# Two more pairs of a two-layer fp32 chain in seven products: first layer's pairs 3 and 4 in two phases, products summed in PSUM

## The chip, the cores and the metric

One core of one Trainium2 chip. The time is that of one execution on the device, in microseconds, median over several. TensorE (PE) multiplies; ScalarE (ACT) and VectorE (DVE) read and write what PE leaves in PSUM; GpSimd (POOL) only fills small tiles; SyncE (SP) issues every DMA from one queue, in order. Each engine works through its own list in the order in which it was built.

## The reference

```
q_s = exp(q - max(q, -1)) / (sum + 1e-9)          # over the head's 64 columns
k_s = exp(k - max(k, axis=2)) / (sum + 1e-9)      # over the 576 positions
x   = q_s @ (k_s^T @ v)                           # 8 batches, 8 heads, 576 x 64
x   = [4608, 512]                                 # heads side by side
h   = x @ w_in1 ; g = h * sigmoid(1.702 h) ; x = g @ w_out1     # 512 -> 2048 -> 512
h   = x @ w_in2 ; g = max(0.01 h, h)       ; x = g @ w_out2
```

q, k and v are float32; the four weight matrices come as float64 and are turned into float32 on the chip. All of it is kept at float32 accuracy.

## The kernel before

The 4608 rows are nine chunks of 512 (0 to 8). Float32 factors are cut into a high and a low half (`split_hi` on ACT, `split_lo` on DVE) and each 128x128x512 product is made of three matmuls: high-high, low-high, high-low. A hidden stripe of 128 columns is an f (0 to 15), two of them a quad (n = 0 to 7).

Layer 1 (index 0 in the code) begins with chunks 0 and 1, one after the other, while attention and weight conversion run beside them. Then come pairs of chunks: pair 2 (chunks 2 and 3), pair 3 (4, 5), pair 4 (6, 7), and chunk 8 alone (`single`). Layer 2 has four pairs and chunk 8 alone. For a pair, the first product takes seven products of blocks for eight (Winograd's form of Strassen): the pair is cut into a11, a12, a21, a22, s1 to s4 are sums of these, and the weights' sums t1 to t4 are built once and stored (`wq`).

There are two ways to run a pair. In layer 1, `pair_first` makes the quads (`quad_step`, line 896) and, beside each, the second product of the first chunk (`g2`, line 789, eight of eight blocks); `pair_second` then makes the second chunk's second product. A quad step is 42 matmuls of L732 and 24 of L789. In layer 2, `quad_apart` (line 947) makes all quads alone, keeping g of both chunks in SBUF, and `pair_apart` then makes the second product in seven rounds (`ROUNDS`) of four pages, each page 12 matmuls (L1056): 336 for a pair instead of 384. For each page `prepare` casts a high half (ACT `sh`), subtracts for the low half (DVE `sl`), and in the first three rounds makes one more DVE subtraction for a later round.

Attention goes by units (chunk c, pair of heads j), pipelined over three ticks by class `Units`, one tick beside each quad: `kma` and `kmb` (transposes for the column maximum), `qtp` (transposes of q), `kvp` (k^T v), `pxt` (the product with q), with q's exponentials on ACT (`q1b`) and k's maximum and subtraction on DVE. Weights of layer 2 are converted by `conv_step`, 33 steps of two ACT and four DVE instructions (L109, L112; L116, L117, L126, L130), spread over layer 1's pairs 3 and 4.

PSUM has eight banks: three named h, acc0 to acc3, and one named att. In `quad_step` the first block a goes to SBUF (`p`, L905) and DVE adds it to b and c (L900). A gap list (`gaps[0..9]`) says beside which block each extra piece is issued, and a scheduler then orders each engine's list.

## Time and profile before

| | us |
|---|---|
| median of three runs | 1624.9 (1624.11 to 1628.83) |
| the profiled execution | 1628.65 |
| its span | 1626.9 |
| PE busy in the span | 1587.7 |
| first quad of pair 3 begins | 440.79 |
| first quad of pair 4 begins | 634.19 |
| first matmuls of chunk 8's first product (`h`) | 807.50 |

PE is busy in almost all of the span after the first 200 us. A busy PE says only that matmuls are in flight; whether it is at its pace is read from the start of one group of matmuls to the start of the next. The times of the stages above are starts of matmuls in the timeline of PE.

### The profile page before, as it was taken

How to read it: one execution, taken by the hardware profiler on the slowest of the kernel's cores; microseconds unless marked ns; L12 is line 12 of the kernel's file. 1: busy time of each engine (PE TensorE's matmuls, PEld its weight loads, DVE VectorE, ACT ScalarE, POOL GpSimd, SP SyncE). 2: the span in 40 equal slices, each digit the busy share in tenths (PEclk: the TensorE clock that was granted, in tenths of full speed). 3: DMA queues.
4: the chain of work that ended last, by engine and by line, in shares of the span. 5: the costliest groups of instructions: out<-in, count | busy, mean ns of one | idle time of the engine just before them, and what ended most of it. 6: DMA issues, size and time to landing. Idle time of an engine off the chain costs nothing.

```text
span 1626.9 us, 22121 instructions
## 1 busy us (share of the span) xinstructions
PE 1587.7 (98%) x7632; PEld 1268.3 (78%) x7632; DVE 1053.7 (65%) x1623; ACT 800.9 (49%) x1698; POOL 35.2 (2%) x162
## 2 busy tenths in 40 slices
PE   5999999999999999999999999999999999999998
PEld 3677778777877778778888888788888888888887
DVE  7899659786776757667544666644774487547411
ACT  7787656556545655445333545333453354334422
POOL 1000000000000002000000000000000000000000
PEclk9999999999999999999999999999999999999999
DMA  8788577778788887978896977996776777676763
GB/s 215 226 274 256 167 234 269 255 247 262 249 281 264 260 260 243 303 253 281 306 330 228 321 272 264 316 292 203 242 209 203 233 212 215 194 230 195 223 192 102
DMA packets 221775, 397.84 MB, mean 245 GB/s; under 512 B 57568, under 2 KB 138464, under 8 KB 221664
## 3 DMA queue, kind: packets, MB, share of 16 engines
q1 hardware_dynamic: 221664, 396.43, 76.1%
q8 instruction: 61, 1.00, 0.3%
q14 instruction: 50, 0.41, 0.1%
HBM read 306.18 MB, written 90.18 MB: 244 GB/s over the span
## 4 chain that ended last, share of the span: by engine, by line
PE 77%; DVE 7%; DMA 7%; issue 3%; ACT 1%; SPq 1%; ACTq 0%; DVEq 0%; POOL 0%; POOLq 0%
PE acc L789 23%; PE hb L732 13%; PE ha L732 9%; PE hc L732 8%; PE h L719 7%; PE ob L1056 6%; PE oa L1056 4%; PE oc L1056 4%; DMA o<-cv 2%; PE pxt L556 2%; DMA wo<-wp 1%; DMA w<-cv 1%; DVE cv L126 1%; DVE gl L86 1%; DMA raw<-in_moe_w_in_dram 1%
## 5 line engine op out<-in xcount | busy, mean ns | idle before, releaser
L789 PE MATMUL acc<-gh,wo 128*128 128x512 f32 x1152 | 362.8, 396 | 2.6 <-ACT wo L83 1.8
L789 PEld LDWEIGHTS acc<-gh,wo 128*128 128x128 f32 x1152 | 211.5, 188 | 48.9 <-ACT wo L83 2.2
L789 PE MATMUL acc<-gl,wo 128*128 128x512 f32 x576 | 225.6, 392 | 0.0
L719 PE MATMUL h<-x,wi 128*128 128x512 f32 x768 | 191.3, 399 | 2.8 <-ACT wi L83 2.8
L719 PEld LDWEIGHTS h<-x,wi 128*128 128x128 f32 x768 | 144.2, 191 | 37.2 <-ACT wi L83 4.4
L732 PE MATMUL ha<-x,wa 128*128 128x512 f32 x624 | 161.8, 393 | 2.8 <-ACT p L905 2.8
L732 PEld LDWEIGHTS ha<-x,wa 128*128 128x128 f32 x624 | 115.6, 188 | 33.0 <-issue 5.7
L83 ACT CAST sh<-a 128x1024 fp32r<-128x1024 f32 x84 | 88.2, 1050 | 94.4 <-PE oc L1056 35.1
L86 DVE TENSOR_TENSOR sl<-a,sh 128x1024 fp32r<-128x1024 f32 x84 | 102.7, 1222 | 49.4 <-ACT sh L83 49.0
L789 PEld LDWEIGHTS acc<-gl,wo 128*128 128x128 f32 x576 | 108.3, 188 | 23.8 <-issue 0.8
L956 DVE TENSOR_TENSOR a<-hb,a 128x512 f32<-128x512 f32 x72 | 49.7, 690 | 91.3 <-PE hb L732 91.3
L732 PE MATMUL hb<-x,wc 128*128 128x512 f32 x384 | 97.4, 389 | 0.0
L508 ACT ACTIVATE qt<-qt,qmx 128x64 f32<-128x64 f32 x256 | 86.0, 338 | 13.0 <-DVE qmx L498 12.2
L1056 PE MATMUL ob<-sh,wo 128*128 128x512 f32 x288 | 91.7, 394 | 0.0
L732 PE MATMUL hb<-xb,wb 128*128 128x512 f32 x336 | 86.1, 390 | 0.0
L83 ACT CAST gh<-gb 128x512 fp32r<-128x512 f32 x80 | 49.3, 617 | 71.8 <-PE acc L789 69.6
L732 PEld LDWEIGHTS hb<-x,wc 128*128 128x128 f32 x384 | 72.1, 188 | 14.9
L789 PE MATMUL acc<-wo,gh 128*128 128x512 f32 x256 | 79.2, 390 | 1.3 <-DMA wo<-wp 1.3
L83 ACT CAST gh<-gf 128x512 fp32r<-128x512 f32 x96 | 59.1, 616 | 42.5 <-DVE gf L757 33.6
L86 DVE TENSOR_TENSOR gl<-gb,gh 128x512 fp32r<-128x512 f32 x80 | 54.7, 687 | 35.5 <-ACT gh L83 34.2
L86 DVE TENSOR_TENSOR gl<-gf,gh 128x512 fp32r<-128x512 f32 x96 | 65.9, 687 | 18.0 <-ACT gh L83 17.1
L753 ACT ACTIVATE a<-a 128x512 f32<-128x512 f32 x72 | 45.5, 632 | 64.2 <-DVE a L956 64.2
(182 smaller groups left out, 2842.2 us busy)
## 6 DMA issues: line engine op xcount, KB each, us to landing
wo<-wo SPq DMA_DIRECT2D x144, 512.0 KB, 4.6
wo<-wp SPq DMA_DIRECT2D x68, 512.0 KB, 3.6
wo<-wt SPq DMA_DIRECT2D x48, 512.0 KB, 3.6
wa<-wq SPq DMA_DIRECT2D x40, 512.0 KB, 4.0
wb<-wq SPq DMA_DIRECT2D x40, 512.0 KB, 4.2
wc<-wq SPq DMA_DIRECT2D x40, 512.0 KB, 4.7
raw<-in_moe_w_in_dram SPq DMA_DIRECT2D x32, 512.0 KB, 4.9
raw<-in_moe_w_out_dram SPq DMA_DIRECT2D x32, 512.0 KB, 4.9
```

Of the source, the lines that this page charges most:

```text
L83: nc.scalar.copy(hi, src)
L86: nc.vector.tensor_tensor(out=lo, in0=src, in1=hi.bitcast(F32), op=ALU.subtract)
L126: nc.vector.scalar_tensor_tensor(out=w[:, o], in0=hw, scalar=0xC0000000, in1=w[:, o], op0=ALU.bitwise_and, op1=ALU.bitwise_or)
L508: nc.scalar.activation(t[:, h, r, :], t[:, h, r, :], AF.Exp, bias=mx[:, h, r : r + 1], accum_out=sm[:, h, r : r + 1],)
L556: nc.tensor.matmul(pv[o, :, a:e], kvb[b, j][o, :], t[o, :, a:e], start=True, stop=True)
L719: nc.tensor.matmul(h, WI[f][:, b, wh, o * P : (o + 1) * P], xs[f"a{side}{b + 1}"][xh][:, o, :], start=(i == 0), stop=(i == n - 1),)
L732: nc.tensor.matmul(h, w[:, wh, o * P : (o + 1) * P], xo[xh][:, o, :], start=(start and i == 0), stop=(i == 5), skip_group_check=not start,)
L753: nc.scalar.activation(t, h, AF.Prelu, alpha=0.01)
L789: nc.tensor.matmul(acc[d], lhsT, rhs, start=(f == 0 and i == 0), stop=(f == NF - 1 and i == 2))
L956: add = lambda out, h, t: nc.vector.tensor_tensor(out=out, in0=h, in1=t, op=ALU.add)
L1056: nc.tensor.matmul(banks[name][d], w[:, l, wh, sl], x[:, l, :], start=first_one, stop=(m == NQ // 2 - 1 and l == 1 and i == 2), skip_group ...
```

## The change

Pairs 3 and 4 of layer 1 go the way of layer 2: `quad_apart`, then `pair_apart`, both now with layer 1's activation and its factor of 0.5. Attention for chunks 6, 7 and 8 goes by a new class `LateUnits`, one tick beside each quad of the first phase: the transposes `kma` and `kmb` between the blocks, and `qtp`, `kvp` and `pxt` one behind the other at the quad's end. Its results go to DRAM (`x_store`) and come back for the next pair. The blocks a and b are summed in PSUM: ACT copies a into b's bank (and the first part of b or c to SBUF) and the later matmuls accumulate on it, in `quad_step`, `quad_apart` and `pair_apart`; the quads rotate over five banks. Three matmuls (`hp`) are added ahead of pair 2. The sums of w_out1 that the seven products need are built and stored (`sum_pieces(0, ...)`) during the first stage and pair 2, and the first stage stores w_out1 twice. `conv_step` moves: one step in each of pair 3's and 4's quads, three in pair 3's pages, nine in pair 4's, five in chunk 8. The sums for layer 2 are built in chunk 8 and in layer 2's first pair. Quads of odd number take their weights through the `wo` tiles, pages of the first four rounds through the `wi` tiles.

PE, one quad step of pair 3 before (names: ha, hb, hc are the three banks; what stands behind the arrow are tiles of x and of weights), up to the transposes of q:

```order
L732 MATMUL ha<-x,wa 128x512 x6
L732 MATMUL hb<-xb,wb 128x512 x6
L446 MATMUL kma<-ident,kmx 128x128
L732 MATMUL hc<-x,wb 128x512 x6
L732 MATMUL ha<-x,wa 128x512 x6
L732 MATMUL hb<-xb,wc 128x512
L456 MATMUL kmb<-ident,km 128x128
L732 MATMUL hb<-xb,wc 128x512 x5
L732 MATMUL hc<-xb,wd 128x512 x6
L532 MATMUL qtp<-ident,qs 128x128 x4
```

The same list after the change, from the second block of a quad of pair 3 to the first block of the next:

```order
L784 MATMUL hc<-x,wb 128x512 x6
L482 MATMUL kma<-ident,kmx 128x128
L784 MATMUL hb<-xb,wb 128x512 x6
L784 MATMUL ha<-x,wa 128x512 x6
L784 MATMUL hb<-xb,wc 128x512 x6
L492 MATMUL kmb<-ident,km 128x128
L784 MATMUL hc<-xb,wd 128x512 x6
L784 MATMUL hb<-x,wc 128x512 x6
L575 MATMUL qtp<-ident,qs 128x128 x4
L513 MATMUL kvp<-vt,kt 64x65 x10
L601 MATMUL pxt<-qT,kv_5104 64x4x112 x2
L601 MATMUL pxt<-qT,kv_5705 64x4x16 x2
L784 MATMUL ha<-x,wo 128x512 x6
```

What was in five places is in three: between the transposes of q and the next quad stood 24 matmuls of L789 and a block, and the seven blocks now stand alone.

DVE, in the pages of pair 4 (layer 1) after the change: `sl` is the low half for one page, the L654 row a subtraction for a later round, `cv` the conversion of a weight tile:

```order
L91 TENSOR_TENSOR sl<-a_6691,sh 128x1024
L654 TENSOR_TENSOR a_6691<-a_6692,a_6689 128x1024
L121 TENSOR_SCALAR cv_7533<-cv_7533 128x512
L122 TENSOR_SCALAR cv_7533<-cv_7533 128x512
L131 SCALAR_TENSOR_TENSOR cv_7533<-raw_7491,cv_7533 128x512
L91 TENSOR_TENSOR sl<-a_6889,sh 128x1024
L135 ISA cv_7533<-cv_7533 128x1024
L654 TENSOR_TENSOR a_6889<-a_6890,a_6887 128x1024
L91 TENSOR_TENSOR sl<-a_7109,sh 128x1024
L91 TENSOR_TENSOR sl<-a_7293,sh 128x1024
L654 TENSOR_TENSOR a_7109<-a_7110,a_7107 128x1024
L654 TENSOR_TENSOR a_7293<-a_7294,a_7291 128x1024
```

Before, such pages were in layer 2 alone and held no conversion; there the list ran so:

```order
L86 TENSOR_TENSOR sl<-a_10541,sh 128x1024
L602 TENSOR_TENSOR a_10541<-a_10543,a_10541 128x1024
L86 TENSOR_TENSOR sl<-a_10672,sh 128x1024
L602 TENSOR_TENSOR a_10672<-a_10674,a_10672 128x1024
L86 TENSOR_TENSOR sl<-a_10281,sh 128x1024
L602 TENSOR_TENSOR a_10281<-a_10282,a_10279 128x1024
```

So four instructions of a conversion now stand among the low halves that the pages wait for.

SP, while chunk 8 of layer 1 runs alone, after the change (`wi` and `wo` are the weights of one f, `raw` a tile to convert, `o_4..`/`w_..` stores and loads of weight tiles, `wt` stores of sums):

```order
L324 DMA wo<-wp_1_133 128x1024
L273 DMA w_8293<-o_0_124 128x1024
L319 DMA wi<-wq_4_88 128x1024
L324 DMA wo<-wp_1_137 128x1024
L319 DMA wi<-wq_4_88 128x1024
L98 DMA raw_8336<-in_moe_w_in_dram 128x4x128
L215 DMA o_7_131<-cv_8290 128x512
L273 DMA w_8346<-o_1_125 128x1024
L324 DMA wo<-wp_1_133 128x1024
L296 DMA wt_0_152<-wt 512x1x256
L296 DMA wt_0_152<-t_8339 512x1x256
L319 DMA wi<-wq_5_89 128x1024
```

and before:

```order
L309 DMA wo<-wo_97 128x1024
L303 DMA wi<-wq_3_81 128x1024
L309 DMA wo<-wo_98 128x1024
L303 DMA wi<-wq_4_82 128x1024
L262 DMA w_8314<-o_2_128 128x1024
L309 DMA wo<-wo_99 128x1024
L285 DMA wt<-wt 512x1x256
L285 DMA wt<-t_8307 512x1x256
L303 DMA wi<-wq_4_82 128x1024
L309 DMA wo<-wo_100 128x1024
L303 DMA wi<-wq_5_83 128x1024
L309 DMA wo<-wo_101 128x1024
```

The loads of an f are the same; behind them stand two more rows of a conversion in every second f, and the sums' rows are closer together.

The diff, cut to its core:

```diff
@@ load_quad, load_wo, load_round
-        t = new_wi("w" + "abcd"[m])
+        if n % 2:
+            t = wi_view(new_wo(0).rearrange("p l n -> p (l n)"))
+        else:
+            t = new_wi("w" + "abcd"[m])
...
-        src = wod[f].rearrange("p (h n) -> p h n", h=2) if i == 0 else wpd[m][:, n, :, :]
-        nc.sync.dma_start(out=WO[f].bitcast(F32), in_=src)
+        nc.sync.dma_start(out=WO[f].bitcast(F32), in_=wpd[i][m][n // 2][:, n % 2, :, :])
...
+    def load_round(i, k):
+        r, m = ROUNDS[k // (NQ // 2)][0], k % (NQ // 2)
+        if k < 2 * NQ:
+            t = new_wi("wr").rearrange("p b h d -> p (b h d)")
+        else:
+            t = new_wo(0).rearrange("p l n -> p (l n)")
+        t = t.rearrange("p (l h d) -> p l h d", l=2, h=2)
         if r[0] == "t":
-            src = wtd[:, int(r[1]) - 1, ns, :, :]
+            src = wtd[i][m][:, int(r[1]) - 1, :, :, :]
         else:
             o = 2 * P * (int(r[2]) - 1)
-            src = wpd[int(r[1]) - 1][:, ns, :, o : o + 2 * P]
...
@@ c4: what the first stage stores of each w_out tile
-            nc.sync.dma_start(out=wod[f], in_=WO[f].rearrange("p h n -> p (h n)").bitcast(F32))
+            nc.sync.dma_start(out=wpd[0][f % 2][f // 4][:, f // 2 % 2, :, :], in_=WO[f].bitcast(F32))
+            nc.sync.dma_start(out=o32d[0][f // 2][:, f % 2, :], in_=w)
...
@@ bank, pin, k7
+    roomy = False
+
+    def pin(ins):
+        if roomy:
+            tc.keep_in_program_order(ins)
...
+        if roomy and name in OWN_BANKS:
+            return ps.tile([P, T], F32, tag=f"acc{OWN_BANKS.index(name)}", name=name, bufs=1)
...
+        if roomy:
+            nc.vector.tensor_scalar_mul(kv, pk[:, 0:D], rs)
+        else:
+            nc.scalar.activation(kv, pk[:, 0:D], AF.Copy, scale=rs)
...
@@ x_store
+    def x_store(c, j):
+        t = ev_tile()
+        nc.scalar.copy(t, x.pop((c, j)))
+        nc.sync.dma_start(out=xd[0][c][:, j, :], in_=t)
...
@@ LateUnits.tick
+            if b:
+                if b[0] < B:
+                    at(2, k2, *b)
+                    at(2, k3, *b)
+                at(1, q2, *b)
+                at(3, self.load, "q")
+                if b[0] < B:
+                    at(5, k4, *b)
+                    at(5, k5, *b)
+                    at(5, k5b, *b)
+                at(8, q3, *b)
+                if b[0] < B:
+                    at(8, k6, *b)
+            if c:
+                at(8, x_product, *c)
+            if b:
+                if b[0] < B:
+                    at(8, k7, *b)
+                    at(8, self.load, "v")
+                    at(8, self.load, "k")
+                at(8, q4, *b)
+            if c:
+                at(8, x_store, *c)
+            if a:
+                if a[0] < B:
+                    at(5, k1, *a)
+                at(3, q1, *a)
+                at(4, q1b, *a, (0,))
+                at(7, q1b, *a, (1,))
...
@@ quad_apart
-        a = ps.tile([P, T], F32, tag="h", name="ha", bufs=3)
+        a, c, b = (
+            ps.tile([P, T], F32, tag=tag, name=f"h{x}", bufs=3 if tag == "h" else 1)
+            for x, tag in zip("acb", (("h", "h", "h", "acc2", "acc3") * 3)[3 * (n % 5) :])
+        )
         product(a, "a11", W["w11"], True)
-        nc.scalar.copy(t21, a)
+        with tc.high_priority(offset=URGENT):
+            nc.scalar.copy(b, a)
         run(gaps[1])
-        b = ps.tile([P, T], F32, tag="h", name="hb", bufs=3)
-        product(b, "s2", W["t2"], True)
-        add(t12, b, t21)
+        product(c, "s1", W["t1"], True)
+        with tc.high_priority(offset=URGENT):
+            nc.scalar.copy(t22, c)
         run(gaps[2])
-        c = ps.tile([P, T], F32, tag="h", name="hc", bufs=3)
-        product(c, "s1", W["t1"], True)
-        add(t22, c, t21)
+        product(b, "s2", W["t2"], False)
+        with tc.high_priority(offset=URGENT):
+            nc.scalar.copy(t12, b)
         run(gaps[3])
         product(a, "a12", W["w21"], False)
         act1(layer, a, t11)
+        act2(layer, a, t11)
         run(gaps[4])
         product(b, "s3", W["t3"], False)
-        add(t22, b, t22)
-        act1(layer, t22, t22)
+        h22 = pool["cv"].tile([P, T], F32, tag="v5", name="h22", bufs=2) if layer == 0 else t22
+        add(h22, b, t22)
+        act1(layer, h22, t22)
+        act2(layer, h22, t22)
         run(gaps[5])
         product(c, "s4", W["w22"], False)
-        add(t12, c, t12)
-        act1(layer, t12, t12)
+        h12 = pool["cv"].tile([P, T], F32, tag="u2", name="h12", bufs=2) if layer == 0 else t12
+        add(h12, c, t12)
+        act1(layer, h12, t12)
+        act2(layer, h12, t12)
         run(gaps[6])
         run(gaps[7])
         product(b, "a22", W["t4"], False)
-        add(t21, b, t21)
-        act1(layer, t21, t21)
+        act1(layer, b, t21)
+        act2(layer, b, t21)
...
@@ pair_apart
             h = banks[name]
+            if r == 0:
+                banks["b"] = acc2("b")
+            elif r == 1:
+                v5 = tmp("v5")
+            elif r == 3:
+                u2 = tmp("u2")
             for d in range(2):
                 if r == 0:
-                    if d == 0:
-                        p1 = tmp("p1")
-                    nc.scalar.copy(p1[d], h[d])
+                    nc.scalar.copy(banks["b"][d], h[d])
                 elif r == 1:
-                    if d == 0:
-                        v5 = tmp("v5")
-                    add(v5[d], h[d], p1[d])
+                    take_out(v5[d], h[d])
                 elif r == 3:
-                    if d == 0:
-                        u2 = tmp("u2")
-                    add(u2[d], h[d], p1[d])
-                elif r == 2:
-                    t = pool["cv"].tile([P, T], F32, tag="ev", name="ev", bufs=4)
-                    nc.scalar.copy(t, h[d])
-                    out_part(c, d, t)
+                    take_out(u2[d], h[d])
                 elif r == 4:
                     add(v5[d], h[d], v5[d])
-                    out_part(c + 1, 2 + d, v5[d])
+                    out_part(layer, c + 1, 2 + d, v5[d])
                 elif r == 5:
                     add(u2[d], h[d], u2[d])
-                    out_part(c, 2 + d, u2[d])
+                    out_part(layer, c, 2 + d, u2[d])
                 else:
-                    add(p1[d], h[d], p1[d])
-                    out_part(c + 1, d, p1[d])
+                    t = ev_tile()
+                    take_out(t, h[d])
+                    out_part(layer, c if r == 2 else c + 1, d, t)
 
...
@@ second_steps, work_apart
+    def work_apart(layer, c, n, gaps):
+        if n + 1 < NQ:
+            for i, m in zip((1, 3, 5, 7), (0, 1, 2, 3)):
+                if (layer, n + 1, m) not in ahead:
+                    gaps[i].append(lambda m=m: load_quad(layer, n + 1, m))
+        else:
+            for i in range(3):
+                gaps[2 * i + 1].append(lambda i=i: fetched.append(load_round(layer, i)))
+        if layer == 0:
+            for i, piece in zip((3, 6, 8), conv_step()):
+                gaps[i].append(piece)
...
@@ main loop
+    hi = XO["a11"][0]
+    for i in range(3):
+        h = ps.tile([P, T], F32, tag="h", name="hp", bufs=3)
+        nc.tensor.matmul(h, hi[:, 0, 0:P], hi[:, 0, :], start=True, stop=True)
...
+            units = LateUnits(chunks_of(*nxt)) if layer == 0 else None
+            if units:
+                for what in "kqkvqv":
+                    units.load(what)
+            roomy = layer == 0
             for n in range(NQ):
-                gaps = empty()
-                work(n, gaps)
+                gaps = units.tick() if units and units.busy else empty()
+                work_apart(layer, c, n, gaps)
                 quad_apart(layer, n, gaps)
-            pair_apart(c, second_steps(None, nxt), fetched)
+            roomy = False
+            ahead = []
+            steps = second_steps(units, nxt)
+            if layer == 0:
+                for k in (1, 5, 9) if c == 4 else range(0, 27, 3):
+                    spread(steps, conv_step(), k, 1, 27)
+            pair_apart(layer, c, steps, fetched)
+            if nxt == (0, LAST):
+                give("cv", "lo", "at", "g")
+                take("left", "lo", "cv", "wt")
+                take("right", "sb", "gb")
+                split, narrow[0] = False, False
...
-                for f in (0, 3, 6, 9, 11, 13):
-                    spread(steps, conv_step(), f)
+                spread(steps, sum_pieces(0, range(SUMS, NQ)), 0)
             else:
-                spread(steps, sum_pieces(range(SUMS, NQ)), 0)
...
+            give("wt", "cv", "lo", "gb", "sb")
+            if layer == 0:
+                give("at")
+            take("left", "lo", "cv")
+            take("right", "g")
+            if layer == 0:
+                take("right", "at")
+            else:
+                evs[0] = 4
+            split = True
         elif layer == 0:
...
@@ the single chunk of the first layer
+                if f % 2 == 0 and f < 10:
+                    pieces_of_step[:] = conv_step()
+                for piece in pieces_of_step[:1 + f % 2]:
+                    piece()
+                del pieces_of_step[:1 + f % 2]
+                if f >= 4:
                     sum_steps.pop(0)()
```

## Rows read from the trace of the kernel before

**Rows 1.** The page, busy time, and the chain of waits by engine

```profile
PE 1587.7 (98%) x7632; PEld 1268.3 (78%) x7632; DVE 1053.7 (65%) x1623; ACT 800.9 (49%) x1698; POOL 35.2 (2%) x162
...
PE 77%; DVE 7%; DMA 7%; issue 3%; ACT 1%; SPq 1%; ACTq 0%; DVEq 0%; POOL 0%; POOLq 0%
```

**Rows 2.** Chain in order of time, chunk 8 of layer 1: start, length, what

```profile
818.54 2.72 PE h L719 x12
821.26 2.72 PE acc L789 x12
```

**Rows 3.** What PE waited for, 430 to 810 us: total, times, longest

```profile
PE pxt L556 <- ACT kv L492: 2.9, 3, 1.2
PE ha L732 <- ACT p L905: 2.8, 2, 2.4
PE hb L732 <- DVE u L900: 0.8, 1, 0.8
```

**Rows 4.** Timeline of PE, one quad step of pair 3: start, length, what

```profile
551.77 1.66 PE L732 MATMUL ha<-x,wa 128*128 128x512 f32 x6
553.26 1.52 PE L732 MATMUL hb<-xb,wb 128*128 128x512 f32 x6
554.62 0.27 PE L446 MATMUL kma<-ident,kmx 128*128 128x128 f32 x1
...
569.67 1.66 PE L732 MATMUL ha<-x,wa 128*128 128x512 f32 x6
```

**Rows 5.** Timeline of ACT in that stage: exponentials, then steps back to back

```profile
532.01 0.33 ACT L508 ACTIVATE qt<-qt,qmx 128x64 f32<-128x64 f32 x1
...
532.34 0.33 ACT L508 ACTIVATE qt<-qt,qmx 128x64 f32<-128x64 f32 x1
...
559.33 0.66 ACT L109 ACTIVATE cv<-raw 128x512 uint32<-128x512 uint32 x1
...
561.50 0.57 ACT L540 COPY qT<-qtp 128x512 f32<-128x512 f32 x1
```

**Rows 6.** Groups of DVE instructions by form: times, busy us, mean ns, idle

```profile
L126 DVE SCALAR_TENSOR_TENSOR cv<-raw,cv 128x512 uint32<-128x512 uint32 x64 | 43.9, 685 | 0.4
L130 DVE CUSTOM_DVE_ANT_0 cv<-cv 128x1024 uint16<-128x1024 uint16 x64 | 43.8, 684 | 5.7 <-ACT cv L109 5.3
L429 DVE TENSOR_REDUCE kmx<-kt 128x128 f32<-128x640 f32 x28 | 36.3, 1296 | 15.2 <-DMA kt<-in_k_dram 15.0
L116 DVE TENSOR_SCALAR cv<-cv 128x512 f32<-128x512 f32 x64 | 27.2, 424 | 41.7 <-ACT cv L112 41.7
L117 DVE TENSOR_SCALAR cv<-cv 128x512 uint32<-128x512 uint32 x64 | 26.8, 419 | 0.6
L462 DVE TENSOR_TENSOR kt<-kt,kmb 128x640 f32<-128x640 f32 x28 | 22.8, 815 | 9.1 <-PE kmb L456 8.6
```

**Rows 7.** Timeline of DVE, pages of layer 2: start, length, what

```profile
1165.08 1.22 DVE L86 TENSOR_TENSOR sl<-a,sh 128x1024 fp32r<-128x1024 f32 x1
1166.33 1.22 DVE L602 TENSOR_TENSOR a<-a,a 128x1024 f32<-128x1024 f32 x1
1167.47 1.22 DVE L86 TENSOR_TENSOR sl<-a,sh 128x1024 fp32r<-128x1024 f32 x1
```

**Rows 8.** Windows: busy us (and count) by engine; last PE clock, DMA share, GB/s

```profile
825.00:850.00 25.00, 25.00 (x112) 20.71 (x111) 11.47 (x19) 7.47 (x11) 0.00 (x0) 1.00 0.97 336
1025.00:1050.00 25.00, 24.03 (x106) 19.29 (x105) 12.96 (x20) 8.02 (x11) 0.00 (x0) 1.00 0.98 331
440.00:637.00 197.00, 191.35 (x1010) 149.89 (x1009) 138.36 (x242) 106.40 (x274) 13.77 (x33) 1.00 0.84 264
637.00:807.00 170.00, 168.12 (x739) 134.09 (x738) 111.59 (x177) 72.85 (x132) 0.23 (x1) 1.00 0.84 281
1150.00:1175.00 25.00, 25.00 (x114) 20.47 (x113) 22.21 (x20) 11.28 (x13) 0.00 (x0) 1.00 0.63 192
```

**Rows 9.** What PE waited for over the whole span

```profile
PE acc L789 <- DMA wo<-wp: 1.3, 3, 0.5
```

377 lines of the change are left out of this document (216 added, 161 removed).

## The prediction

> **What bounds the kernel now.** I read the busy times and the chain of waits first [rows 1]: PE is busy 98% of the span and 77% of the chain is PE's own work, so the time is the number of matmuls by their pace, plus what little PE waits. The pace is read where nothing disturbs it, in chunk 8 of layer 1 [rows 2]: twelve matmuls in 2.72 us, 0.2267 us each. Next, what PE waits for in pairs 3 and 4 [rows 3]: 2.9 + 2.8 + 0.8 = 6.5 us, for ACT and DVE on tiles that the change does away with or on attention whose place it changes. The timeline of one quad step [rows 4] gives what attention costs PE: from one first block to the next 569.67 - 551.77 = 17.90 us, of which 66 matmuls of the chain are 14.96, so 2.94 us are attention and what it disturbs. The windows [rows 8] say how near the other limits are: the mean over pairs 3 and 4 is a DMA share of 0.84 at 264 and 281 GB/s, DVE is busy 138.36 of 197 us and ACT 106.40; in layer 2's pages DVE is at 22.21 of 25 us; and the two stretches nearest to a full DMA are 336 GB/s at 0.97 and 331 at 0.98. So PE bounds pairs 3 and 4, with DMA and DVE not far behind, and the change takes from PE and gives to DMA and DVE.
>
> **Parts, one by one.** The sum goes against the profiled execution's 1628.65 us, which is 3.75 above the median; it is brought to the median's scale at the end.
>
> 1. Matmuls. The second product of a pair goes from 384 to 336, twice: -96. Three `hp` are added: -93 by 0.2267 = -21.1 us. That holds where PE is the bound, and PE is at its pace there (busy 191.35 of 197 us and 168.12 of 170) [rows 8].
>
> 2. Bursts of other matmuls. Behind a burst the next block takes longer: in [rows 4] the first block lasts 553.26 - 551.77 = 1.49 us, the second 1.36; 0.13 a burst. A quad with attention has five such places before and three after: 2 x 0.13 x 8 quads of pair 3 = -2.1. Ends: 0 (the block is slow for another reason) and -4 (pair 4's units save as much).
>
> 3. Waits that go. The wait on `p` and the wait on `u` [rows 3] belong to tiles that are gone: the first block is copied into the bank of b, and the later matmuls add to it. The wait of `pxt` on `kv` goes too, since `pxt` now multiplies what a unit of the quad before left. -6.5. Ends: 0 and -6.5.
>
> 4. Waits that come in pair 3's first phase. Without the 24 matmuls beside them, a quad is 42 x 0.2267 + 2.94 - 0.26 = 12.2 us of PE, and a whole attention unit must fit it. ACT: 8 exponentials of 0.33 and some 12 other instructions of 0.54 (four steps in 561.50 - 559.33) [rows 5] = 9.2 us. DVE [rows 6]: a conversion 0.685 + 0.684 + 0.424 + 0.419 = 2.2, the two steps on k 1.30 and 0.82, and some ten half steps of 0.68 make 11.1. DMA: 3.74 MB a quad, counted from SP's list, 306 GB/s over 12.2 us, below 336. Each fits, DVE with 1 us to spare. The chain within a quad is what can be late: `qtp`, a copy by ACT, `kvp`, `pxt`, now back to back with only the next quad behind them. The trace has no such burst; the nearest row is the wait on `kv` [rows 3], at most 1.2 us. Ends: 0 and 8 x 1.0 = 8. I take +3, nearer to none, since `pxt` has a whole quad of distance from its `kv`.
>
> 5. DVE in the pages of pairs 3 and 4. A page is 2.72 us of PE [rows 2]; its `sl` and the subtraction for a later round take DVE 1167.47 - 1165.08 = 2.39 [rows 7]. Each conversion adds 2.2. In pair 4, three to four conversions fall in the first ten pages: 23.9 + 3.5 x 1.9 = 30.5 us against 27.2 of PE, with about 0.9 of lead: 2.4 late, given back nowhere, since PE is idle meanwhile; pair 3 with three conversions in all its pages, 0.5. Later pages have no subtraction, and DVE catches up. I take +3. Ends: 0 (the pages' tiles give more lead) and 7 (nine conversions by 0.8).
>
> 6. DMA in pair 4's pages and chunk 8. SP's list has there 27.3 + 30.1 = 57.4 MB (tiles of 128x1024 are 0.524 MB), and PE 336 + 384 matmuls, 163 us: a need of 352 GB/s. The fullest rows are 336 and 331 [rows 8]; at these it takes 171 to 173 us, 8 to 10 late. Tiles fetched ahead of the first page cover a part of that, and every stretch that isn't full adds to it. Ends: 0 and 12, which is 328 GB/s. I take +5, the middle, since two rows just below the need say that it is close to the limit. The only waits of this kind before are `acc` on `wo`, 1.3 us in all [rows 9].
>
> The Trainium skill ("DMA: Bandwidth & Descriptors", section "Bandwidth") gives 425 GB/s for a single core's long transfer and 341 for one of 1 MB; by the first, the 57.4 MB would take 135 us, an estimate from that page, and this term would be nothing; by the second it stands. The rows with a share of 0.97 at 336 agree with the second figure.
>
> 7. Passages from pair 2 to 3, 3 to 4, 4 to chunk 8. Before, the second chunk's product of one pair ran while the next one's tiles came; now `x_store` rows stand in SP's queue ahead of the loads of k, q and v, and the next pair's first block waits for tiles that return from DRAM. Nothing like it is in the trace; nearest are the waits for a transfer, 1.3 us for three [rows 9]. Ends 0 and 5; I take +1.5.
>
> 8. The first stage stores w_out1 twice and builds its sums: 4.2 MB more at the start and 4.7 MB and about 9 us of DVE, where DVE and DMA stand beside a PE that waits for attention. Ends 0 and 4; I take +1. The rotation over five banks, `k7` on DVE and the conversion steps in quads I cost at nothing: they are in the DVE and ACT sums of part 4, which cover them; without that cover they would be part 4's upper end.
>
> Sum: -21.1 - 2.1 - 6.5 + 3 + 3 + 5 + 1.5 + 1 = -16.2, so 1612.4 on the profiled execution's scale and 1612.4 x 1624.9 / 1628.65 = 1608.7, say 1608. With all added terms at 0 it is 1595; with all at their upper ends (+36) and parts 2 and 3 at 0, about 1639.
>
> **Rivals.**
>
> B. Transfers don't bind in pair 4's pages and chunk 8. For it: SP may run ahead in tiles of three kinds, and the need of 352 is little over what the rows show. Against: both rows at 0.97 or more are below the need. Then part 6 is nothing: 1603. The figure of 425 in the Trainium skill's page named above speaks for this; no row here shows it.
>
> C. Attention sets pair 3's pace. The unit that was spread over five places and 17.90 us of a quad must go through ACT and DVE in 12.2. For it: DVE has 1 us to spare by my sum, and any order in its list that puts a conversion ahead of `kt` makes `kmb` and the block after it late. Against: ACT has 3 us to spare. With quads of 14 us instead of 12.2, 8 x 1.8 = 14.4 in place of part 4's 3: 1608 + 11 = 1619 to 1620, the edge of no change.
>
> D. Slower. Transfers bound pairs 3 and 4 and chunk 8 throughout. SP's list has 25.2 + 24.1 + 20.2 + 27.3 + 30.1 = 126.9 MB from pair 3's first quad to the end of chunk 8. At the mean rate of [rows 8] in these stages, 264 and 281, so 273, that is 465 us. PE needs 97.6 for the eight quads, 76.2 for each of the two sets of pages, some 80 for pair 4's quads and 87.1 for chunk 8, with 4 at the passages 421: so it ends 44 us late: 1595 + 44 = 1639. It decides from a rate of 126.9 MB / (421 + 31) us = 281 GB/s down: above it the change is still faster. For it: from pair 3 to chunk 8 the kernel before moved no more than this on average. Against: PE was the bound there and asked for no more, and the rows at 336 and 331 show the rate that it has when asked.
>
> E. It does better: the waits of parts 4, 5, 7 and 8 stay near nothing and part 6 small, 1593 to 1597. For it: before, PE lost no more than 6.5 us to such waits in these stages [rows 3]. Against: each of the five has less room than before.
>
> **How the numbers follow.** What can be told from no change is 0.3%, 4.9 us: 1620.0 to 1629.8. Chances: the forecast of 1608, with its own range 1598 to 1616, 0.52; B 0.17; E 0.09; C 0.12, of which half falls within 0.3% of no change; D 0.07, and 0.03 for sums of parts 4 to 8 that end within 0.3%. Faster: 0.52 + 0.17 + 0.09 + 0.06 = 0.84; same 0.06 + 0.03 = 0.09; slower 0.07. The range from 1594 to 1621 leaves out D, half of E and a little of C.
>
> **What the profile after would show.** Step 1: PE's count down by 93, and a page in pairs 3 and 4 every 2.72 us. Steps 2 to 4: pair 3's quads 12.2 us apart; no wait of `ha` or `hb` on ACT but the copy into b's bank; `pxt`, `kvp` and `qtp` waiting under 0.4 us a quad. C is right where they are 14 us apart. Step 5: waits of pages on DVE `sl`, a few us in pair 4 and almost none in pair 3. Step 6: from the first page of pair 4 to the end of chunk 8, a DMA share near 1 and waits on `wi` and `wo` of some 5 us; with share near 1 and none, B; with such waits from pair 3's first quads on, D. Step 7: idle PE at the three passages of under 2 us in all. My forecast is wrong if the first quad of pair 3 comes over 4 us late (step 8), or if waits in pairs 3 and 4 and chunk 8 add up to over 25 us.

## The result and the profile after

The changed kernel takes 1643.57 us (median of four runs, 1642.99 to 1646.68), the kernel before beside it 1626.58 (1624.11 to 1628.83): a ratio of 1.0109, 95% interval 1.0087 to 1.0131. It is 17 us slower. 1608 was forecast, with 1594 to 1621 as the range, and slower had a chance of 0.07.

The page of after, busy times and the chain by engine, to stand against [rows 1]:

```profile
PE 1579.3 (96%) x7539; PEld 1251.6 (76%) x7539; DVE 1022.7 (62%) x1508; ACT 898.8 (55%) x1833; POOL 30.8 (2%) x162
...
PE 58%; issue 10%; DMA 7%; DVE 6%; ACT 3%; SPq 1%; POOL 0%; ACTq 0%; DVEq 0%; POOLq 0%
```

The 93 matmuls are gone from PE's count. But PE's share of the chain fell from 77% to 58%: the end no longer hangs on the number of matmuls alone. The waits of PE that the trace lists add up to 59.9 us over the span, 34.9 before.

Where the time is, by PE's first matmul of each stage (the parts of pair 3 and 4 have no counterpart before, only their sums have; layer 2 is counted to its last matmul). The rows are of one profiled execution each, 1646.68 us after, the longest of its four, and 1628.65 before:

| us | before | after |
|---|---|---|
| pair 3 begins | 440.79 | 457.82 |
| pair 3 (quads + pages after) | 193.4 | 110.9 + 86.7 |
| pair 4 (quads + pages after) | 173.3 | 88.1 + 81.1 |
| chunk 8 | 87.0 | 85.3 |
| layer 2 | 727.8 | 730.4 |

Before begins pair 3 with 24 matmuls of pair 2 still open (5.4 us), so 11.6 of the first line's 17.0 are a loss. Pairs 3 and 4, where 96 matmuls (21.8 us) left, take 366.8 us, where before took 366.7 with those 5.4 in them.

The windows of after by these stages (stretch, length; PE, PEld, DVE, ACT, POOL busy; granted clock, DMA share, GB/s), to stand against [rows 8]:

```profile
457.80:568.70 110.90, 99.14 (x567) 75.45 (x565) 78.54 (x142) 72.90 (x219) 6.96 (x32) 0.97 0.88 257
568.70:655.40 86.70, 82.83 (x379) 64.68 (x380) 71.31 (x81) 46.19 (x56) 0.00 (x0) 1.00 0.83 278
655.40:743.50 88.10, 85.35 (x369) 64.77 (x368) 59.74 (x94) 56.88 (x146) 1.62 (x4) 1.00 0.81 266
743.50:824.60 81.10, 79.45 (x341) 62.91 (x340) 66.70 (x79) 44.63 (x57) 0.00 (x0) 1.00 0.86 293
824.60:909.90 85.30, 81.92 (x358) 66.67 (x357) 56.48 (x91) 37.74 (x58) 0.00 (x0) 1.00 0.90 316
```

PE stands still 11.8 us in pair 3's quads (110.90 - 99.14) and 3.9 in its pages. A quad there takes 110.9 / 8 = 13.9 us, not 12.2. No other engine and no DMA window is full. What PE waited for from 457 to 570 us, the two longest (total, times, longest), beside [rows 3]:

```profile
PE ha L784 <- DMA wo<-wq: 4.7, 2, 2.6
PE hc L784 <- DMA wo<-wq: 2.6, 3, 1.1
```

Both are weights that come late, though DMA isn't full. SP's own waits in these quads say why:

```profile
SPq L104 <- DVE cv L131: 19.4, 3, 8.1
SPq L98 <- DVE cv L131: 13.3, 3, 5.3
```

SP's timeline at the longest of them (start, length, transfer):

```profile
530.30 0.43 SPq L310 DMA_DIRECT2D wc<-wq  x1
538.84 0.33 SPq L104 DMA_DIRECT2D raw<-in_moe_w_out_dram  x1
539.22 0.43 SPq L308 DMA_DIRECT2D wd<-wq  x1
...
545.16 0.56 SPq L310 DMA_DIRECT2D wo<-wq  x1
545.76 1.15 SPq L389 DMA_DIRECT2D qt<-in_q_dram  x2
546.96 0.90 SPq L310 DMA_DIRECT2D wo<-wq  x2
```

The load of `raw`, the next float64 tile to convert, goes into the tile that DVE's step L131 is still reading. It stood at the head of SP's queue until 538.84, and the 14 transfers behind it in these rows, four of them weights, went out only then. PE met them here:

```profile
551.46 2.01 PE L784 MATMUL ha<-x,wo 128*128 128x512 f32 x6 [2.65 <-DMA wo<-wq]
554.58 2.93 PE L784 MATMUL hc<-x,wo 128*128 128x512 f32 x6 [1.11 <-DMA wo<-wq]
```

So the first theory was: the loss is the place of such rows in SP's queue. The rival: it is the new work itself, the sums of w_out1 and the conversions, wherever its rows stand.

### The profile page after: what moved, and what is told of

Its sections match the earlier page's. It is cut to its first block, busy times and chain, and to the rows that moved or that the text cites. A ratio compares the mean times of both kernels' runs of the same rounds, so it can differ in the third digit from the quotient of the medians.

```text
span 1644.7 us, 21908 instructions
## 1 busy us (share of the span) xinstructions
PE 1579.3 (96%) x7539; PEld 1251.6 (76%) x7539; DVE 1022.7 (62%) x1508; ACT 898.8 (55%) x1833; POOL 30.8 (2%) x162
## 4 chain that ended last, share of the span: by engine, by line
PE 58%; issue 10%; DMA 7%; DVE 6%; ACT 3%; SPq 1%; POOL 0%; ACTq 0%; DVEq 0%; POOLq 0%
PE acc L843 13%; PE hb L784 11%; PE hc L784 7%; PE ha L784 7%; PE ob L1211 6%; PE oc L1211 4%; PE oa L1211 4%; PE h L771 4%; DMA wo<-wp 2%; DMA w<-cv 1%; DMA o<-cv 1%; ACT qt L549 1%; DMA wb<-wq 1%; DMA wt<-t 1%; PE pxt L601 1%
## 5 line engine op out<-in xcount | busy, mean ns | idle before, releaser
L91 DVE TENSOR_TENSOR sl<-a,sh 128x1024 fp32r<-128x1024 f32 x140 | 171.1, 1223 | 76.1 <-ACT sh L88 75.6
L843 PE MATMUL acc<-gh,wo 128*128 128x512 f32 x640 | 204.9, 400 | 8.8 <-DMA wo<-wp 4.9
L843 PEld LDWEIGHTS acc<-gh,wo 128*128 128x128 f32 x640 | 118.0, 190 | 36.9 <-ACT gf L805 3.1
L843 PE MATMUL acc<-gl,wo 128*128 128x512 f32 x320 | 125.9, 394 | 0.0
L784 PE MATMUL ha<-x,wa 128*128 128x512 f32 x384 | 101.4, 395 | 0.9 <-DMA wa<-wq 0.6
L1211 PE MATMUL oa<-sh,wr 128*128 128x512 f32 x320 | 98.6, 390 | 1.0 <-ACT qT L585 1.0
L654 DVE TENSOR_TENSOR a<-a,a 128x1024 f32<-128x1024 f32 x60 | 73.1, 1223 | 1.3
L1211 PEld LDWEIGHTS oa<-sh,wr 128*128 128x128 f32 x320 | 59.8, 188 | 13.6 <-ACT qT L585 1.1
L784 PE MATMUL ha<-x,wo 128*128 128x512 f32 x240 | 62.4, 394 | 4.7 <-DMA wo<-wq 4.7
L784 PE MATMUL hb<-xb,wo 128*128 128x512 f32 x240 | 63.1, 399 | 2.7 <-ACT hb L1095 1.8
```

Source lines behind the costliest of these rows:

```text
L91: nc.vector.tensor_tensor(out=lo, in0=src, in1=hi.bitcast(F32), op=ALU.subtract)
L654: nc.vector.tensor_tensor(out=out, in0=a, in1=b, op=ALU.subtract)
L784: first = nc.tensor.matmul(h, w[:, wh, o * P : (o + 1) * P], xo[xh][:, o, :], start=(start and i == 0), stop=(i == 5), skip_group_check=no ...
L843: nc.tensor.matmul(acc[d], lhsT, rhs, start=(f == 0 and i == 0), stop=(f == NF - 1 and i == 2))
L1211: nc.tensor.matmul(banks[name][d], w[:, l, wh, sl], x[:, l, :], start=first_one, stop=(m == NQ // 2 - 1 and l == 1 and i == 2), skip_group ...
```

## Experiments: the queue, the sums, pair 4 alone, PSUM

Each ratio is to the kernel before, run beside it in five rounds, with a 95% interval. 0.1% is 1.6 us.

**e1**: the load of `raw` goes to the end of the quad.

```diff
-            for i, piece in zip((3, 6, 8), conv_step()):
+            for i, piece in zip((3, 6, 8, 9), conv_step(True)):   # last piece: d0, the load of raw
```

> The changed kernel with one DMA moved: in the quads of pairs 3 and 4 the load of the next tile to convert (raw) stands behind the next quad's weights, k, v and x rows in SP's queue instead of ahead of them. Theory Q (SP's queue): that load waits for DVE to be done with the tile before it (5 to 8 us a time in pair 3), and the weights of the next quad wait behind it; the 8.2 us that PE waits for weights in pair 3's quads and the some 3.5 us at a lowered clock behind the longest of these waits go: 1643.6 - 11 = about 1632. Rival A (attention's chain through ACT and DVE sets pair 3's pace): the waits turn into others, 1641 to 1645.

1.0082 [1.0065, 1.0099]. In the trace the waits all but went (the same view and stage as above):

```profile
PE hb L784 <- DMA wo<-wq: 0.5, 1, 0.5
...
PE hc L784 <- DMA wo<-wq: 0.3, 1, 0.3
```

and pair 3's quads took 101.6 us. But the ratio is only 0.27% lower, some 4 us of the 17, and its interval still meets that of after: the waits were real, and not the most of the loss.

**e2**: no sums in layer 1.

```diff
-            nc.sync.dma_start(out=o32d[0][f // 2][:, f % 2, :], in_=w)
-            first_sums = sum_pieces(0, range(SUMS))
-            load_blocks(0, 0)
+            first_sums = []
```

> The changed kernel without the sums of w_out1: none are built or stored in the first stage and pair 2 (the second store of w_out1 is gone too), and the pages of layer 1 load plain blocks of w_out1 in their place, as many bytes; so layer 1's result is another. Theory S (the sums' DVE, ACT and DMA work makes pair 3 begin late): pair 3's first quad comes some 10 us earlier, 1643.6 - 10 = about 1633. Rival P (the copies into PSUM, the three hp matmuls and the new order of blocks make it late): at most 2 us earlier, 1641 to 1644.

0.9971 [0.9958, 0.9985]: 22.4 us less than after (1.38% of 1627). How much work that was, the pages say (e2, then after; the busy times of after stand above):

```profile
PE 1575.6 (97%) x7539; PEld 1250.9 (77%) x7539; DVE 1000.1 (62%) x1468; ACT 890.8 (55%) x1825; POOL 30.5 (2%) x162
...
DMA packets 244717, 399.91 MB, mean 246 GB/s; under 512 B 57728, under 2 KB 167296, under 8 KB 244608
```

```profile
DMA packets 244334, 416.70 MB, mean 253 GB/s; under 512 B 58368, under 2 KB 159744, under 8 KB 244224
```

The sums and the second store are 22.6 us of DVE, 8.0 of ACT and 16.8 MB. Pair 3 begins at 447.42, PE's row in e2 against that in after:

```profile
447.42 0.84 PE L786 MATMUL ha<-x,wa 128*128 128x512 f32 x3
```

```profile
457.82 0.39 PE L784 MATMUL ha<-x,wa 128*128 128x512 f32 x1
```

10.4 us of the 22.4 are lost before pair 3. By the third quad of pair 2 it was 5.1 (293.06 against 288.01). The other 12 are in and behind pair 3, whose quads are 99.2 us in e2, though no sum is built there any more (the last is stored at 455).

**e3**: pair 3 as before, pair 4 in two phases.

```diff
+                for f in (0, 3, 6, 9, 11, 13):          # pair 3's second product
+                    spread(steps, conv_step(), f)
...
+                held = pair_second(layer, c + 1, steps)
```

> The changed kernel with pair 3 run as before (its second product beside its quads, 48 matmuls more, attention spread over the gaps, five wi tiles), pair 4 in two phases. Theory Q: pair 3 loses its 15 us of excess and gets 10.9 us of matmuls back, the sums' cost stays: 1643.6 - 4 = about 1640, and pair 4 keeps its own excess of about 6 us. Rival D (transfers bind pair 4 and chunk 8 for themselves): the time saved in pair 3 is lost behind it, 1643 or more.

1.0090 [1.0066, 1.0113], about as after: only half of the matmuls go, and pair 2 and the first stage still carry the sums.

**e4**: before, with sums kept in PSUM in `quad_step` and the three `hp`.

```diff
-        nc.scalar.copy(p1, a)
+        nc.scalar.copy(b, a)
```

> The kernel before with one part of the change: quad_step adds a, b and c in PSUM by ACT's copy, and the three hp matmuls stand ahead of pair 2. Both theories: the waits for p and u (3.6 us in the profile of before) go and 0.7 us come, about 1624 against 1626.6 before. Rival P (the copies into PSUM delay the blocks behind them): 1628 or more.

1.0024 [1.0012, 1.0035]: this part gives nothing by itself, it takes 4 us (2 to 6).

## Experiments: can the sums be hidden?

**e5**: e3, with all sums in pair 3's second product instead of in the first stage and pair 2. **e6**: e5 with `quad_step` as before.

```diff
+                pieces = [p for k, p in enumerate(sum_pieces(0, range(NQ))) if k % 3 < 2]
+                spread(steps, pieces + kept, 0)
```

> Pair 3 as before and pair 4 alone in two phases, as in the run with pair 4 only, but the sums of w_out1 are all built in pair 3's second product (none in the first stage or in pair 2's second product, which has six conversion steps again). Theory S (it is the place of the sums that costs: they stand where DVE and the DMAs are full): the some 10 us in which pair 3 begins late come back, little is lost in pair 3, 0.9% over before becomes 0.3% over to 0.2% under. Rival (the sums cost the same wherever they stand): 0.7 to 1.0% over before.

> The same with the kernel before's quad_step (the first block goes to SBUF, DVE adds it) in pairs 2 and 3 and layer 2's first pair, and without the hp matmuls. Theory C (ACT's copy into the bank, behind the exponentials in its list, makes blocks late): 0.2% faster than the run it starts from. Rival (that run's loss of 0.24% with copies alone came from elsewhere): the same within 0.1%.

1.0206 [1.0192, 1.0220] and 1.0195 [1.0177, 1.0212]. The sums went over into pair 4's quads, where PE waited 17.6 us in e5:

```profile
PE hb L784 <- DVE h L1082: 17.6, 5, 14.9
```

So this place isn't free either. The two differ by less than their intervals, so this place doesn't tell what the step in PSUM is worth.

**e7**: after, with the sums of `quad_apart` in SBUF on DVE, as before.

```diff
-            nc.scalar.copy(b, a)
...
+            p1 = t21
...
+            nc.scalar.copy(p1, a)
...
+            add(h22, c, p1)
```

> The changed kernel with the old way of adding blocks in the quads of pairs 3 and 4: ACT copies the first block to SBUF and DVE adds it to the next two and the last; the pages and quad_step stay. Theory C: the waits of hb on ACT's copy go in pairs 3 and 4 (2.6 us listed, some more below what is listed), 3 to 5 us faster than the changed kernel, 0.8 to 0.9% over before. Rival D (DVE has no room): its additions come late and quads get longer, 1.1% over before or more.

1.0128 [1.0113, 1.0144]: no better. Keeping the sums in PSUM isn't the loss in two phases.

**e8**: e1 and e2 together.

> Both edits of the first runs: no sums of w_out1 (layer 1's pages load plain blocks of w_out1 in their place) and the load of the next tile to convert behind the next quad's weights. Theory Q and S: the queue's wait still costs where there are no sums: 0.3% faster than without the sums alone, 0.6% under before. Rival: without the sums, DVE is done with each tile in time and the row's place costs nothing: 0.2 to 0.4% under before.

0.9992 [0.9983, 1.0002], 0.2% above e2, where e1 was 0.27% under after. Without the sums, the later load of `raw` is no gain. In the profiles its place shows only beside the sums: pair 3's quads take 110.9 us in after and 101.6 in e1, 99.2 in e2 and 99.8 in e8.

**e9a**: the sums are made and not stored. **e9b**: they are loaded and stored, and not made.

```diff
-        for j, half in enumerate((h, lo)):
+        for j, half in enumerate((h, lo) if i else ()):        # e9a
...
+        if i == 0:                                             # e9b
+            w = sums.pop((i, n))[0]
+            for j in range(2):
+                nc.sync.dma_start(out=wtd[i][n // 2][:, :, n % 2, j, :], in_=w)
+            return
```

> The changed kernel with the sums of w_out1 loaded and computed but not stored, and layer 1's pages loading plain blocks of w_out1 in their place (so layer 1's result is another): DVE's and ACT's work stays, the sixteen stores of 0.5 MB and their places in SP's queue go. Without any of the sums' work the time was 0.3% under before, with all of it 1.1% over. Theory V (the transfers and their rows in SP's queue): 0.1% under to 0.2% over before. Theory W (DVE's and ACT's work, 3 us a sum): 0.7 to 1.1% over.

> The other half: each piece of w_out1 is loaded and stored twice as it is, with no subtraction and no cast (layer 1's result is another): as many bytes, nothing on DVE and ACT, and no store that waits for a compute engine. Theory V by volume: 0.7 to 1.1% over before. Theory V by waiting rows (a store that waits for DVE holds the weights behind it), or theory W: 0.1% under to 0.3% over.

1.0032 [1.0019, 1.0045] and 1.0072 [1.0054, 1.0091]: +10 us and +16 over e2. This isn't a split into engines and bytes: e9a still stores w_out1 twice and loads the pieces, 8.4 of the 16.8 MB (its page has 408.31), and e9b moves all 16.8. So a half of the bytes is in both, and 10 + 16 is more than 22.4, though within the intervals. Pair 3 begins 4.1 and 6.4 us later than in e2 (PE's rows of e9a, then e9b):

```profile
451.49 0.84 PE L787 MATMUL ha<-x,wa 128*128 128x512 f32 x3
```

```profile
453.84 0.39 PE L793 MATMUL ha<-x,wa 128*128 128x512 f32 x1
```

4.1 + 6.4 is about the 10.4 of e2, but not at the same places. The second quad of pair 2 begins at 269.98 us in e2, 273.97 in e9a, 276.57 in e9b and 275.42 in after: up to there each half costs about as much as both (in kernels with all sums the row lies from 274.68, e13, to 279.46, e1, so it is good to a few us). From the eighth quad of pair 2 to pair 3, where five of the eight sums stand, it takes 69.9 us in e2, 70.0 in e9a and in e9b, and 75.3 in after: there neither half costs anything and both together 5.4. (It is 74.3 to 75.7 us in the nine kernels that have all sums and pair 3 in two phases.) The windows of that stretch, columns as above, in before, e2, e9a, e9b and after:

```profile
380.00:458.00 78.00, 78.00 (x387) 62.72 (x386) 55.19 (x87) 41.36 (x103) 1.92 (x11) 1.00 0.80 254
380.00:458.00 78.00, 78.00 (x387) 62.76 (x386) 39.47 (x56) 32.92 (x61) 0.89 (x7) 1.00 0.69 215
380.00:458.00 78.00, 78.00 (x390) 62.02 (x389) 48.80 (x76) 37.14 (x60) 1.33 (x9) 1.00 0.74 243
380.00:458.00 78.00, 78.00 (x389) 61.92 (x390) 37.21 (x54) 33.48 (x65) 1.82 (x13) 1.00 0.94 309
380.00:458.00 78.00, 74.66 (x366) 58.69 (x366) 47.69 (x75) 36.23 (x62) 1.33 (x9) 0.98 0.86 276
```

A cost that needs both halves points to the sums' rows in SP's queue that wait for the engines. In after, from 385 to 462 us, the loads and stores of the sums do (the first three rows). The loads of PE's weights stand behind them. A load that waits for PE is early: in after that comes 10 times (the fourth row), in e9a, from 382 to 452, 13 times (the last row), and 13 times in e9b and e2 as well.

```profile
SPq L273 <- DVE t L654: 9.7, 4, 3.6
SPq L296 <- DVE t L91: 4.6, 5, 1.3
SPq L296 <- ACT wt L88: 4.1, 2, 3.5
SPq L324 <- PE acc L843: 16.5, 10, 3.4
```

```profile
SPq L324 <- PE acc L846: 27.9, 13, 4.6
```

**e10**: the steps of `LateUnits` from gap 8 to gaps 3 and 5, so that there are five bursts again. **e12**: e1, and the stores of the sums one piece later.

```diff
-                at(8, q3, *b)                 # e10
+                at(3, q3, *b)
+                at(3, q4, *b)
...
-                at(8, x_product, *c)
+                at(5, x_product, *c)
```

```diff
-                lambda: None,                 # e12
+                lambda n=n: sums_store(i, n) if i == 0 else None,
```

> The changed kernel with the attention unit of a quad in five places again: the transposes of q after the third block, the product with q after the fifth, k^T v at the quad's end. Theory B (one burst per quad saves 0.13 us for each place that goes): 2 to 3 us slower than the changed kernel, 1.2 to 1.3% over before. Rival (the burst's parts wait for each other's copies by ACT, and apart they do not): 2 to 4 us faster, 0.8 to 1.0% over.

> The changed kernel with the tile to convert loaded behind the next quad's weights, as in the first run, and each sum's two stores one piece later, when DVE is done with them. Theory Q for both (rows that wait in SP's queue hold weights back): 0.82% over before becomes 0.4 to 0.6%. Rival V by volume or W: 0.8% over, as with the load alone.

e10: 1.0130 [1.0112, 1.0148], e12: 1.0067 [1.0049, 1.0085]. e10 is 0.2% above after, the way that the term for bursts would have it, within the intervals. e12 is just clear of after: the places of rows in SP's queue are worth some 7 us of the 17, give or take 4. It is the best of the kernels that run both pairs in two phases with all the work, and still slower than before. The sums' stores still wait for ACT and DVE in it (5.4 and 3.7 us), and the stretch before pair 3 still takes 74.3 us.

## Experiments: attention and conversions

**e13**: no attention in pairs 3 and 4 (x comes from a weight tile). **e15**: no conversions; layer 2 takes layer 1's weights. **e16**: neither. **e17**: the kernel before, no conversions.

```diff
-            units = LateUnits(chunks_of(*nxt)) if layer == 0 else None     # e13, e16
+            units = None
...
-        if n > 2 * NF:                                                     # e15, e16, e17
-            return []
+        return []
```

> The changed kernel without the attention of chunks 6 to 8 (their x is read from other stored data, so their results are another). In the kernel before, this attention costs PE 2.94 us in each of pair 3's eight quads, 4.3 in its second product and some 8 in pair 4, 36 us or 2.2%. Theory B (in the new staging it costs PE no more than there): 1.1% over before becomes 1.1% under. Theory E (the unit's chain through ACT, DVE and SP's queue costs PE another 10 to 18 us in the new staging): 1.7 to 2.2% under.

> The changed kernel without the 33 conversion steps of layer 2's weights (layer 2 takes layer 1's weights, so its result is another): their DVE and ACT work, loads and stores go from pairs 3 and 4 and chunk 8; every other load stays. Theory K (the conversions take what room the two-phase pairs have: the rows of raw in SP's queue, sl in the pages, chunk 8's transfers): 12 to 18 us, 0.0 to 0.4% over before. Rival (only the row's place in the queue mattered): 4 to 7 us, 0.7 to 0.85% over.

> Both left out, what the first two runs leave out each. If the two costs are separate, the sum of the two reductions; if they are the same loss (the two chains delay each other on DVE, ACT and in SP's queue), less by the part that they share, 5 us or more.

> The kernel before without its conversion steps (layer 2 takes layer 1's weights). There PE waits 6.5 us in all in pairs 3 and 4. Theory K: conversions lie beside matmuls there, so 0 to 4 us faster (0 to 0.25% under), and the changed kernel's loss by them is the new staging's. Rival: they cost as much there as in the changed kernel.

0.9905 [0.9890, 0.9921], 0.9920 [0.9906, 0.9933], 0.9725 [0.9712, 0.9738], 0.9967 [0.9954, 0.9979]. Against after, e13 gains 2.04% and e15 1.89%, together 3.93%, and e16 gains 3.84%: attention and conversions don't stand in each other's way, each costs on its own. Attention's 2.04% are 33 us, no more than the 36 that it cost PE before by the expectation: the new staging doesn't make it dearer. Pair 3's quads in the windows of e15, then e16, then e13:

```profile
458.80:554.50 95.70, 94.44 (x567) 74.08 (x565) 66.26 (x117) 65.98 (x203) 6.72 (x31) 1.00 0.87 265
```

```profile
459.80:535.90 76.10, 76.10 (x337) 63.05 (x336) 39.14 (x54) 34.20 (x57) 0.00 (x0) 1.00 0.71 234
```

```profile
457.40:540.00 82.60, 78.29 (x338) 62.41 (x337) 53.72 (x82) 41.67 (x71) 0.00 (x0) 1.00 0.82 275
```

With neither, 76.1 us are the 336 matmuls at 0.2267 and PE never stands still. With attention alone a quad is 95.7 / 8 = 12.0 us: the forecast's 12.2. With conversions alone, on quads with no attention, 6.5 us are lost: 4.3 as idle PE, the rest as blocks that last longer. How, is in ACT's timeline of e13, and in PE's beside it:

```profile
487.29 0.60 ACT L810 ACTIVATE a<-hb 128x512 f32<-128x512 f32 x1
489.86 0.66 ACT L117 ACTIVATE cv<-raw 128x512 f32<-128x512 f32 x1 [1.97 <-DMA o<-cv]
490.42 0.58 ACT L1100 COPY hb<-ha 128x512 f32<-128x512 f32 x1
```

```profile
488.45 1.52 PE L789 MATMUL hc<-x,wo 128*128 128x512 f32 x6
491.05 1.66 PE L789 MATMUL hb<-xb,wo 128*128 128x512 f32 x6 [1.08 <-ACT hb L1100]
```

ACT's step L117 of the conversion waits 1.97 us until the tile that was converted before has been stored, since both use the same two buffers. The copy into b's bank stands behind it in ACT's list, and PE behind the copy. In before ACT had its copy (`p`) behind such steps as well, but 24 other matmuls in each quad [rows 4]; that these cover the wait is not shown apart. The conversions cost 5.4 us there (e17), 30.7 in after (e15).

**e18**: the steps of a conversion later in the quad, so that nothing in ACT's list should wait for the store, and the later stores of e12.

```diff
+            gaps[4].append(lambda k=cq["stored"]: d3(k))
...
+            gaps[4].append(lambda: d0(k))
+        gaps[7].append(lambda: d1(k))
+        gaps[9].append(lambda: d2(k))
```

> The changed kernel, all of its work, with the conversion in the quads of pairs 3 and 4 placed anew: ACT's two steps behind the sixth block instead of the third (so that they stand behind the copies into the banks in ACT's list, and the store of the tile before has a quad's time to land), DVE's at the quad's end, the store and the next load in the middle of the next quad; and each sum's stores one piece later. Theory L (ACT's list is held at a conversion step that waits for the last tile's store to land, and the copy into b's bank stands behind it: the hb waits of 0.4 to 1.2 us; and SP's queue at raw): 0.67% over before with rows of SP moved alone becomes 0.1 to 0.4% over. Rival (the conversions cost by their mere work and bytes): 0.6 to 0.8% over.

1.0129 [1.0110, 1.0147], over both theories. Pair 3's quads took 101.1 us, where e12 had 101.0, and pair 4 178 us, 169 in after. In its quads and pages PE waited most for

```profile
PE hb L791 <- DVE h L1089: 4.9, 3, 2.6
```

The wait went from ACT's list to DVE's: at 713.24 us DVE's `h` stands behind L121, L122 and L131 of a conversion, and PE waits 1.36 us for it. The place shown in e13 is not the only one. That the order in the lists is the cause of the conversions' whole cost is not shown: the run that was to take the cost away by order didn't.

**e19**: e2 and e15 together.

> The changed kernel with neither the sums of w_out1 nor the conversion of layer 2's weights (both layers' results are others). Against the kernel before without conversions (0.33% under before) it shows what the two-phase staging gives by itself. If matmuls and what else the forecast counted for the staging hold (21.1 + 8.6 us of gains, a few of cost): 1.4 to 1.8% under that, so 1.7 to 2.1% under before. Rival (the staging has costs of its own, transfers or passages): 1.0% under that or less, 1.3% under before.

0.9834 [0.9816, 0.9852]. Against e17, also without conversions, that is 0.9867: -21.7 us. The expectation for gains that hold was 1.4 to 1.8% under e17, and this is 1.3%.

## Why the prediction was wrong

With e2, e15, e17 and e19 the 17.7 us (by the ratio, of 1627) can be split. Each ratio is good to some 0.15%, so a term to about 3.5 us, and the one for both at once to 5.

| us against before | sums made | no sums |
|---|---|---|
| conversions made | +17.7 | -4.7 |
| no conversions | -13.0 | -27.0 (before without: -5.4) |

| term | forecast | runs |
|---|---|---|
| two phases in themselves | -25.2 (parts 1 to 4 and 7) | -21.7 (e19 to e17) |
| sums and the second store | +1 | +14.0 (e15 - e19) |
| conversions, beyond their 5.4 in before | +3 (part 5) | +16.9 (e19: 22.3) |
| both at once | 0 | +8.4 |
| DMA in pair 4's pages and chunk 8 | +5 | within the above |
| sum | -16.2 | +17.6 |

**The steps that held.** Part 1: the matmuls' 21.1 us come off where the new work is left out (-21.7). Part 4's 12.2 us a quad were 12.0 in e15, so a whole attention unit does fit one. Part 3: `p` and `u` are gone from the waits, but that their 3.6 us were gained is not shown: e4, which has this part alone, lost 4. Part 2 is not separated (e10). Part 6: chunk 8's waits on `wo` came to 3.4 us, and the stretch from the first page of pair 4 to the end of chunk 8 took 909.9 - 743.5 = 166.4 us, where 163 were PE's; before, the waits on `wo` were 1.3 [rows 9] and, on the tiles of w_out1, another 0.7. Of the 57.4 MB only 50.7 moved in it (81.1 us at 293 GB/s, 85.3 at 316); the rest lay outside it.

The fullest slices of after's page are 350 and 348 GB/s over 41 us each. The Trainium skill ("DMA: Bandwidth & Descriptors", section "Bandwidth") gives 425 GB/s for a long transfer and 341 for one of 1 MB. These slices lie just above the second, but shorter stretches come near the first: 10 us of after, and in before 422 GB/s over 5 us at 705.5:

```profile
972.00:982.00 10.00, 10.00 (x45) 8.03 (x45) 3.16 (x5) 5.22 (x9) 0.00 (x0) 1.00 1.03 415
```

So the 336 at a share of 0.97 [rows 8], from which part 6 was worked, was not the most that a full DMA moves. The two stretches differ in their packets (972:982 of after, then 825:850 of before):

```profile
DMA packets 1145, 4.15 MB, mean 415 GB/s; under 512 B 126, under 2 KB 126, under 8 KB 1143
```

```profile
DMA packets 3688, 8.40 MB, mean 336 GB/s; under 512 B 258, under 2 KB 2102, under 8 KB 3687
```

With 57% of the packets under 2 KB, a full DMA moved 336 GB/s, with 11% 415. No run changed the packets alone.

**The step that failed first is part 8**, "I take +1". The runs give 14 to 22 us (e15 to e19, after to e2), 10.4 of them before pair 3 even begins. Two things in it were wrong. The first is what it counted: 4.7 MB and 9 us of DVE are three sums, those of the first stage. The other five, in pair 2's second product, have no term at all. With all eight and the second store it is 16.8 MB, 22.6 us of DVE and 8.0 of ACT (e2), not 8.9 MB and 9 us. The second is the place, "beside a PE that waits for attention". Where the sums stand, PE doesn't wait: before and in e2 it is busy 45.00 us of 180 to 225 and 78.00 of the 78 shown above. So this work stood beside the engine that sets the time, and there the five uncounted sums alone cost 5.4 us. The text's own upper end, 4, was below the answer; the rows to bound it by were 16.8 MB at 264 GB/s = 64 us of DMA and 22.6 us of DVE, beside a PE without idle time. How the 12 us in and behind pair 3 come about stays open in part: pair 3's quads lose most of it where `raw` has its old place (after, against e1).

**The second is in the same part**: the conversion steps in quads "I cost at nothing: they are in the DVE and ACT sums of part 4, which cover them". They were in the sums of busy time, and each sum was below the quad's length. At least a part of what they cost comes from order: in lists that are worked off in order, a step that waits (ACT's L117 for a store, SP's `raw` for DVE) holds what stands behind it. The quad of before had 24 matmuls of another product between the steps that need ACT; a quad of seven blocks has none. How much of the 22 to 31 us is order stays open (e18). The pages were under-priced as well: without attention, conversions cost 3.2 us in pair 3's pages and 5.2 in pair 4's (e13 against e16), 8.4 where part 5 had 3. (Part 5 also took 1.9 us for a conversion that it had just put at 2.2; with 2.2 its 2.4 would have been 3.5.)

**The rivals.** C had the right size, 14 us a quad (13.9), but attention doesn't set that pace: without conversions it fits in 12.0 (e15). Conversions and SP's rows make up the rest; a conversion ahead of attention in a list was among C's reasons. D named 1639 and a rate of 281 GB/s below which the change is slower. Pairs 3 to chunk 8 of after in one window:

```profile
457.80:909.90 452.10, 428.69 (x2009) 334.47 (x2008) 332.77 (x484) 258.34 (x532) 8.57 (x36) 0.99 0.86 280
```

Time and rate are D's, yet its mechanism, a full DMA, isn't in the row: the share is 0.86, and e13 has the same 280 GB/s in 413.4 us. So a low rate need not be the cause; a late queue may lower it too. How much of the conversions' 31 us is their bytes and how much their steps on ACT and DVE was not separated, and for the sums only in part (e9a, e9b). Of my two warning signs the first, pair 3's first quad over 4 us late, is what happened; the second, waits over 25 us from pair 3 to chunk 8, is not (452.1 - 428.7 = 23.4 us of idle PE).

## What to carry to other kernels

Before work is put "beside an engine that waits", look at the very stretch in which it will stand: here PE was busy in all of it, and five of eight pieces had not been counted. When a phase is cut to its bare matmuls, sums of busy time alone don't tell whether side work fits (attention did, conversions didn't); go through each in-order list, SP's too, and ask of every step that waits what stands behind it. And test such a change in a two by two, each suspect left out and both: here most of the gain was there (-21.7 of 25.2), and two side costs took more than it.
